# Attention steps, output blocks and the sums of h in the first channel product of batches 3 to 7, written in another order

## The chip, the core and the metric

The kernel runs on one core of one Trainium2 chip. The metric is the device time in microseconds (us) of one execution. The core has a matrix engine (PE), a vector engine (DVE), an activation engine (ACT), a general engine (POOL) and the engine whose queue issues the DMAs (SP). The engines run their own instruction lists in order and wait for each other with semaphores.

## What is computed

A block-diagonal attention, then a token and channel mixer, then a gated spatial mixer, on 8 batches of 576 tokens and 512 channels, in float32:

```python
scores = scale * np.matmul(q_c, k_c.transpose(0, 1, 2, 4, 3))     # chunks of 64 tokens, 8 heads
attn = softmax(scores); x = np.matmul(attn, v_c)
h = np.maximum(xt @ w_tok1, 0.0) @ w_tok2                         # over tokens, 576 -> 256 -> 576
u = x + h.transpose(0, 2, 1)
u + np.maximum(u @ w_ch1, 0.0) @ w_ch2                            # over channels, 512 -> 1536 -> 512
h = np.maximum(x @ w_in, 0.0); u, v = h[..., :512], h[..., 512:]
v_n = (v - mu) / np.sqrt(var + 1e-06)
v_s = np.einsum('ts,bsd->btd', w_spatial, v_n) + b_spatial[None, :, None]
(u * v_s) @ w_out
```

Every product keeps float32 accuracy: each operand is held as two float16 parts, hi and lo, and each product is three matmuls (hi·hi, hi·lo, lo·hi).

## The kernel before

The batches are worked through one after the other, and each batch has these stages on PE: the **first channel product** (`ch1`, 512 to 1536 channels), the **second** (`ch2`), the **gate stage** (five `gate_v` blocks of 128 tokens, normalised, and four `gate_u` blocks between them), the token product of the next batch (`tok1`, `tok2`), and the spatial product (`spatial`, four blocks). The **output product** of a batch (`proj`, L938, 4 or 5 blocks of 12 matmuls with 512 columns) is made in the next batch, at places where PE would else wait. The **attention** of the next batch runs beside all of it: five groups of 128 tokens (the last has 64), each of 20 small steps.

In batches 3 to 7 (`FIRST_FULL`) both channel products use Strassen's form as Winograd has it, with 7 products in place of 8. `ch1_fast(full, between)` goes through six pairs `p` of channel blocks; iteration `p` holds, in this order on PE, the products A11 and S2 of pair p, S4 and A22 of the pair before, then S1, S3 and A12 of pair p, then, if `between` names p, one output block. A product is 6 matmuls of 288 columns. A bank `a` holds A11 + A12 and, beside it, S2; a bank `d` holds S1 and S3, into which S4 and A22 are added later. So S4 of a pair may start only when DVE has read S1 and S3 out of `d`: at L732 (`vb`) and L733 (`c22`).

After A22, DVE adds the last term for two of the four blocks of h (L713, `c`). ACT applies the relu (L716; L735 and L743 for the other two blocks). `ch2_fast` needs h in seven forms: the four blocks h11, h12, h22, h21 and sums of them. DVE makes these sums at L719 (`t13`, two of them in one instruction) and L720, L721 (`t24`), and `split` makes hi (ACT, L509) and lo (POOL, L510; DVE for the first block) of each. The working tiles share three buffers. PSUM has four double banks, which the products, the output blocks and the attention share; a product waits until somebody has read its bank out.

`ch2_fast` begins with A11 of its two halves q (into banks `ab[q]`); ACT copies the result (`s1b`, L778), and only then may A12 be added into the same bank. It ends with `p34(1)`: DVE (L813) makes the residual sum, ACT (L768) its hi, DVE (L769) its lo, into `xb`, which `gate_v` reads next.

What sets the order: PE's order is written out by hand. The attention steps are issued by a pump: each matmul adds its duration times a factor, `PACE` of the stage, to a clock `slow`, and a step is issued each time the clock has gone 112 us over the number of steps. A step puts its PE part there at once (the scores, L241; the weighted sum of v, L287), and gives its DVE, ACT, POOL and DMA parts to a scheduler, which orders those engines' lists when the kernel is built, with `high_priority` blocks first. Of the attention, DVE has per group the reduce and subtract of the scores (L248, L249), the sums and the norm (L258 to L261), lo of q and k (L232) and of v (L276); ACT has hi of q and k (L229), exp (L253), hi of the probabilities (L266), of v (L273), and the two reads of the bank (L302, L303); POOL has two lo's (L269, L306).

In a gate block ACT applies the relu (L871), DVE makes the statistics (L877, L879, L884), POOL a power (L885), DVE the rest (L886, L887, L890), ACT hi (L893). A `gate_u` block's bank is read by ACT (L920).

Of the kernel before, what the change touches and what calls it, by code (L numbers as in the profile page):

```python
# [10 lines left out]
AF = mybir.ActivationFunctionType  # L11
ALU = mybir.AluOpType
# [14 lines left out]
def mixer_kernel(ctx: ExitStack, tc, qk0, qk, v, wt1, wt2, wc1, wc2, win, wsp, bsp, wout, out):  # L27
# [474 lines left out]
            stack.enter_context(tc.issue_after(ins))  # L502
        return stack

    PACE = {"first": 0.2, "pair": 0.8, "ch1": 1.0, "ch2": 1.3, "gate": 1.0, "tok1": 1.0, "last": 0.3}
    sums = {}

    def split(t, hi, lo, eng=DVE):
# [169 lines left out]
    def new_work(name):  # L678
        return wrk.tile([128, 2, 288], F32, tag="t", name=name)
# [3 lines left out]
    def ch1_fast(full, between):  # L683
        high = tc.high_priority
        ab, cd = {}, {}

        def product(o, p, n, b, start):
            w = weights_of(1, p, n, 0)
            fast_product(o, w, lambda e, k: b[:, e, k], start, True, start)

        def block(p, j):
            return hb[:, p, 0, j], hb[:, p, 1, j]

        def store(c, hi, lo, eng=POOL):
            ACT.activation(out=c, in_=c, func=AF.Relu)
            split(c, hi, lo, eng)

        for p in range(7):
            pace[0] = PACE["first" if p < 1 else "pair"]
            if p < 6:  # L700
                ab[p] = a = new_bank()
                product(a[:, 0], p, A11, xb[:, :, 0:2, T1], True)
                product(a[:, 1], p, S2, tq[1], True)
                with high():
                    ACT.activation(out=s1b[0], in_=a[:, 0, 0:288], func=AF.Copy)
                    DVE.tensor_tensor(out=u2b[p % 2], in0=a[:, 1, 0:288], in1=s1b[0], op=ALU.add)
            if p:
                d, u, xp = cd[p - 1], u2b[(p - 1) % 2], xs[(p - 1) % 2]
                product(d[:, 0], p - 1, S4, xb[:, :, 2:4, T2], False)
                product(d[:, 1], p - 1, A22, tq[3], False)  # L710
                with high():
                    c = xp[:, 1:4:2] if full else new_work("c")
                    DVE.tensor_tensor(out=c, in0=d[:, :, 0:288], in1=spread(u), op=ALU.add)  # L713
                    if full:
                        f = hF[p - 1]
                        ACT.activation(out=c, in_=c, func=AF.Relu)  # L716
                        split(xp[:, 2:4], f[:, 1:3, 0], f[:, 1:3, 1], POOL)
                        t13, t24 = new_work("t13"), new_work("t24")
                        DVE.tensor_tensor(out=t13, in0=xp[:, 1:3], in1=xp[:, 0:2], op=ALU.subtract)  # L719
                        DVE.tensor_tensor(out=t24[:, 0], in0=xp[:, 2], in1=t13[:, 0], op=ALU.subtract)  # L720
                        DVE.tensor_tensor(out=t24[:, 1], in0=xp[:, 3], in1=t24[:, 0], op=ALU.subtract)  # L721
                        split(t13, f[:, 3:5, 0], f[:, 3:5, 1], POOL)
                        split(t24, f[:, 5:7, 0], f[:, 5:7, 1], POOL)
                    else:
                        store(c, hb[:, p - 1, 0, 1:3], hb[:, p - 1, 1, 1:3])
            if p < 6:
                cd[p] = d = new_bank()
                c22 = xs[p % 2][:, 2] if full else c22b[p % 2]
                product(d[:, 0], p, S1, tq[0], True)
                product(d[:, 1], p, S3, tq[2], True)  # L730
                with high():
                    DVE.tensor_tensor(out=vb, in0=d[:, 0, 0:288], in1=u2b[p % 2], op=ALU.add)  # L732
                    DVE.tensor_tensor(out=c22, in0=d[:, 1, 0:288], in1=vb, op=ALU.add)  # L733
                    if full:
                        ACT.activation(out=c22, in_=c22, func=AF.Relu)  # L735
                    else:
                        store(c22, *block(p, 3))
                product(a[:, 0], p, A12, xb[:, :, 2:4, T1], False)
                with high():
                    x1 = a[:, 0, 0:288]  # L740
                    if full:
                        xp = xs[p % 2][:, 0]
                        ACT.activation(out=xp, in_=x1, func=AF.Relu)  # L743
                        split(xp, hF[p][:, 0, 0], hF[p][:, 0, 1], DVE)
                    else:
                        hi, lo = block(p, 0)
                        ACT.activation(out=hi, in_=x1, func=AF.Relu)
                        DVE.scalar_tensor_tensor(out=lo, in0=x1, scalar=0.0, in1=hi, op0=ALU.max, op1=ALU.subtract)
            if p in between:
                between[p]()  # L750

# [240 lines left out]
    with tc.manual_schedule(engines={mybir.EngineType.PE}):  # L992
# [12 lines left out]
        for b in range(B):  # L1005
            x = xTs[b % 2]
            if b == 0:
                pumps[0][1] = 1700.0
            def sum_next():
                with behind():  # L1010
                    todo_sums.pop(0)()

            if b == FIRST_FAST - 1:
                sum_pump([(1, p, vall) for p in range(6)], 2200.0)
            pace[0] = PACE["ch1"]
            for m in range(12 if b < FIRST_FAST else 0):
                if b == 0:
                    w_until(4 + m // 2)
                ch1(m)
            if b >= FIRST_FAST:  # L1020
                early = pend[:2]
                pend = pend[2:]
                ch1_fast(b >= FIRST_FULL, {5 - 3 * k: (lambda i=i: proj(b - 1, i)) for k, i in enumerate(early)})
            pace[0] = PACE["ch2"]
            if b == 0:
                SP.dma_start(out=bB, in_=bsp)
                ACT.activation(out=bB, in_=bB, func=AF.Copy, scale=2.0 ** -5)
            if b == FIRST_FULL - 1:
                sum_pump([(2, p, vall) for p in range(4)], 2000.0)
            if b >= FIRST_FULL:  # L1030
                ch2_fast(x)
            else:
                for ms in ((0, 1), (2,), (3,)) if b == 0 else ((0,), (1,), (2,), (3,)):
                    if b == 0:
                        w_until(10)
                    last = ch2(ms, x)
            if b == FIRST_FAST - 1:
                sum_end()
                stream(SLOTS)
            if b == 0:  # L1040
                w_until(21)
                pumps.pop(0)
                mark = last
                pumps.append([clock[0], 4000.0, held_tick, lambda: wdone[0] < len(W), clock])
            for i in pend[:2]:
                proj(b - 1, i)
            if b == FIRST_FULL - 1:
                sum_end()
                sum_pump([(2, p, hall) for p in range(4, 6)], 4500.0)
            fin = None  # L1050
            pair = [psum1(), psum1()] if b == 0 else []
            for ks in ((0, 1, 2), (3,)):
                for j, ps in enumerate(pair):
                    gate_v_part(ps, j, ks)
            pace[0] = PACE["gate"]
            middle = 0 < b < B - 1
            for n, j in enumerate((0, 4, 1, 2, 3) if middle else range(5)):
                f = gate_v(j, pair[j] if j < len(pair) else None)
                if fin:
                    fin()  # L1060
                fin = f
                if middle and n:
                    gate(n - 1)
            if middle:
                fin()
            if b == B - 1:
                fin()
            if not middle:
                for m in range(4):
                    gate(m)  # L1070
            if b < B - 1:
                a_until(b + 1)
                pumps[:] = pumps[1:]
                pace[0] = PACE["tok1"]
                last = tok1()
                attention_from(b + 2, 0.0, 112000.0)
                if b == 0:
                    with tc.issue_after(last):
                        fin()
                pace[0] = PACE["last"]  # L1080
                for m in range(4):
                    tok2(m, xTs[(b + 1) % 2], fast=b + 1 >= FIRST_FAST)
            for i in pend[2:]:
                proj(b - 1, i)
            for m in range(4):
                gated(m, b, DVE if m == 3 and b == B - 1 else POOL)
            if b == FIRST_FULL - 1:
                sum_end()
            if b < B - 1:
                w_until(len(W))  # L1090
                pend = list(range(5 if b % 2 else 4))
# [59 lines left out]
```

## Time and profile before

| | us |
|---|---|
| median of 3 runs | 1165.6 (1165.21 to 1168.64) |
| the profiled execution | 1165.78 |
| its span, first to last instruction | 1164.0 |
| PE busy in it | 1092.1 (94%) |
| DVE, ACT, POOL busy | 776.7, 506.0, 427.8 |

The share of the span lies at 94% on PE, and a busy PE is not yet PE at its peak, since a matmul's record lasts longer than the distance to the next one. So what is to be read is where PE sat idle and what ended the wait.

### The profile page before, as it was taken

The page shows a single profiled execution, that of the slowest core. Times are in us where ns is not written, and L with a number is a line of the kernel's source. Part 1 is how long each engine was busy: PE and PEld are TensorE (multiplying, and loading weights), DVE is VectorE, ACT ScalarE, POOL GpSimd, SP SyncE. Part 2 cuts the span into 40 slices and gives each one's busy share as a digit, 9 for nine tenths or more (in the row PEclk, how much of TensorE's full clock was granted, in tenths as well). Part 3 has the DMA queues.
Part 4 walks back from the last instruction along what each step waited for, and adds up shares of the span by engine and source line. Part 5 has one row for each costly group of instructions (what it writes and reads, how often), then busy time and mean ns, then how long its engine had stood idle before and what let it go on. Part 6 is the DMA issues. An engine that isn't in the chain of part 4 may idle for free.

```text
span 1164.0 us, 26575 instructions
## 1 busy us (share of the span) xinstructions
PE 1092.1 (94%) x10860; PEld 769.7 (66%) x10860; DVE 776.7 (67%) x1269; ACT 506.0 (43%) x884; POOL 427.8 (37%) x392
## 2 busy tenths in 40 slices
PE   5898999999999999988999799987999899999998
PEld 4576757776677755766667575665757676676765
DVE  7999886766565477786568846677556864467332
ACT  3334443534345244563445634455344643346131
POOL 0000032443253453653235533456234552256221
PEclk9899999999999999999999999999999999999999
DMA  9488720564046442456514674246732565124301
GB/s 318 141 250 259 231 73 19 142 160 123 19 115 176 97 114 59 115 143 199 145 39 122 168 200 110 56 132 168 196 101 48 153 153 142 19 84 140 104 19 46
DMA packets 191818, 148.36 MB, mean 127 GB/s; under 512 B 107344, under 2 KB 175696, under 8 KB 189392
## 3 DMA queue, kind: packets, MB, share of 16 engines
q1 hardware_dynamic: 191696, 146.66, 45.4%
q8 instruction: 85, 1.39, 0.5%
q14 instruction: 37, 0.30, 0.1%
HBM read 112.00 MB, written 20.45 MB: 114 GB/s over the span
## 4 chain that ended last, share of the span: by engine, by line
PE 60%; DVE 23%; ACT 5%; issue 5%; DMA 4%; POOL 2%; SPq 1%; DVEq 0%; ACTq 0%; POOLq 0%
PE mp L457 23%; PE mp L667 17%; PE mp L861 7%; PE mp L938 5%; PE mp L835 3%; PE mp L480 3%; DVE t L720 3%; DVE t L721 2%; DVE gb L154 2%; DVE gb L150 1%; DVE qk L232 1%; PE mp L241 1%; PE mp L287 1%; DMA c2s<-vn 1%; DVE gb L148 1%
## 5 line engine op out<-in xcount | busy, mean ns | idle before, releaser
L667 PEld LDWEIGHTS <-c1w 128*128 128x128 f16 x2772 | 269.8, 98 | 110.8 <-issue 40.4
L667 PE MATMUL mp<-xb,c1w 128*128 128x288 f16 x864 | 125.9, 286 | 24.6 <-DVE vn L733 10.7
L835 PE MATMUL mp<-hb,c2w 128*128 128x288 f16 x864 | 110.3, 286 | 4.2 <-DVE c2w L163 2.7
L457 PE MATMUL mp<-spw,vn 128*128 128x288 f16 x896 | 112.8, 286 | 0.0
L457 PEld LDWEIGHTS <-vn 128*128 128x128 f16 x896 | 86.9, 98 | 22.8
L835 PEld LDWEIGHTS <-c2w 128*128 128x128 f16 x864 | 82.8, 98 | 26.7 <-DVE c2w L163 4.0
L667 PE MATMUL mp<-hb,c1w 128*128 128x288 f16 x630 | 90.5, 287 | 9.3 <-ACT vn L778 8.9
L457 PE MATMUL mp<-xb,inw 128*128 128x288 f16 x768 | 98.9, 286 | 0.0
L938 PE MATMUL mp<-otw,gb 128*128 128x512 f16 x432 | 97.3, 379 | 0.0
L861 PE MATMUL mp<-inw,xb 128*128 128x512 f16 x384 | 91.0, 385 | 4.9 <-ACT xb L542 3.5
L457 PEld LDWEIGHTS <-inw 128*128 128x128 f16 x768 | 75.0, 98 | 23.6 <-issue 0.4
L667 PE MATMUL mp<-c2w,c1w 128*128 128x288 f16 x630 | 90.4, 288 | 0.0
L457 PE MATMUL mp<-xb,c1w 128*128 128x288 f16 x576 | 74.8, 290 | 4.4 <-DVE xb L536 2.5
L938 PEld LDWEIGHTS <-gb 128*128 128x128 f16 x432 | 42.2, 98 | 46.4
L457 PEld LDWEIGHTS <-c1w 128*128 128x128 f16 x576 | 56.3, 99 | 20.4 <-issue 2.9
L861 PEld LDWEIGHTS <-xb 128*128 128x128 f16 x384 | 37.3, 99 | 48.1 <-ACT xb L542 4.5
L667 PE MATMUL mp<-c1w 128*128 128x288 f16 x432 | 65.2, 286 | 0.0
L269 POOL TENSOR_TENSOR p<-sd,p 128x512 f16<-128x512 f32 (+1 forms) x30 | 38.9, 1298 | 66.4 <-ACT p L266 55.6
L928 POOL TENSOR_TENSOR gb<-gt,gb 128x576 f16<-128x576 f32 x31 | 41.1, 1327 | 60.2 <-ACT gb L927 60.2
L543 POOL TENSOR_TENSOR xb<-rt,xb 128x576 f16<-128x576 f32 x7 | 10.7, 1533 | 140.1 <-ACT xb L542 140.1
L877 DVE BATCH_NORM_STATS2 st<-vt 128x6 f32<-128x512 f32 (+1 forms) x40 | 27.5, 690 | 45.8 <-ACT vt L871 41.0
L885 POOL TENSOR_TENSOR y<-z,mhalf 128x1 f32<-128x1 f32 (+1 forms) x40 | 24.1, 602 | 92.0 <-DVE z L884 70.0
(236 smaller groups left out, 2018.6 us busy)
## 6 DMA issues: line engine op xcount, KB each, us to landing
c1w<-c1s SPq DMA_DIRECT2D x252, 128.0 KB, 2.4
c1w<-c2s SPq DMA_DIRECT2D x210, 128.0 KB, 2.4
qk<-in_qk SPq DMA_DIRECT2D x96, 128.0 KB, 2.8
out<-o SPq DMA_DIRECT2D x31, 256.0 KB, 2.0
v<-in_v SPq DMA_DIRECT2D x56, 128.0 KB, 2.9
vn<-in_wc SPq DMA_DIRECT2D x4, 1024.0 KB, 4.9
otw<-in_wc SPq DMA_DIRECT2D x3, 1024.0 KB, 4.9
spw<-in_wc SPq DMA_DIRECT2D x3, 1024.0 KB, 5.2
```

Source lines behind the costliest of these rows:

```text
L154: DVE.scalar_tensor_tensor(out=t, in0=w[:, :, 0], scalar=29, in1=t, op0=ALU.logical_shift_right, op1=ALU.bitwise_or)
L269: POOL.tensor_tensor(out=p_hl[rows, 1], in0=m["sd"][rows], in1=p_hl[rows, 0], op=ALU.subtract)
L457: PE.matmul(out=o, lhsT=l, rhs=r, start=(i == 0), stop=(i == len(seq) - 1))
L480: PE.matmul(out=pss[m], lhsT=l, rhs=r, start=(i + j == 0), stop=False)
L667: PE.matmul(out=o[:, 0:288], lhsT=w[:, a, k], rhs=b(e, k), start=(start and k + i == 0), stop=(stop and k == 1 and i == 2), skip_group_che ...
L720: DVE.tensor_tensor(out=t24[:, 0], in0=xp[:, 2], in1=t13[:, 0], op=ALU.subtract)
L835: PE.matmul(out=o, lhsT=c2w[:, a, k, mc], rhs=hb[:, k // 2, r, k % 2 * 2 + t], start=(k + e == 0), stop=(k == 11 and e == 2))
L861: PE.matmul(out=ps, lhsT=l, rhs=r, start=(k + e == 0), stop=(k == 3 and e == len(seq) - 1))
L877: keep("d", DVE.bn_stats(out=st[0:n], in_=t[0:n]))
L885: POOL.tensor_tensor(out=y[0:n], in0=z[0:n], in1=mhalf[0:n], op=ALU.pow)
L928: eng.tensor_tensor(out=gl, in0=t, in1=gh, op=ALU.subtract)
L938: PE.matmul(out=ps, lhsT=gb[:, l, k, tk], rhs=otw[:, r, k], start=(k == 0 and e == 0), stop=(k == 3 and e == 2))
```

## The change

```diff
-    PACE = {"first": 0.2, "pair": 0.8, "ch1": 1.0, "ch2": 1.3, "gate": 1.0, "tok1": 1.0, "last": 0.3}
+    PACES = ({"first": 0.2, "pair": 0.8, "ch1": 1.0, "ch2": 1.3, "gate": 1.0, "tok1": 1.0, "last": 0.3},
+             {"first": 0.0, "pair": 0.2, "ch1": 1.0, "ch2": 1.95, "gate": 1.85, "tok1": 1.5, "last": 0.0})
+    PACE = dict(PACES[0])
...
-                    c = xp[:, 1:4:2] if full else new_work("c")
+                    c = new_work("c")
                     DVE.tensor_tensor(out=c, in0=d[:, :, 0:288], in1=spread(u), op=ALU.add)
                     if full:
                         f = hF[p - 1]
-                        ACT.activation(out=c, in_=c, func=AF.Relu)
+                        ACT.activation(out=xp[:, 1:4:2], in_=c, func=AF.Relu)
+                        t13, t24 = new_work("t13"), new_work("t24")
+                        relu_less = dict(scalar=0.0, op0=ALU.max, op1=ALU.subtract)
+                        DVE.scalar_tensor_tensor(out=t13[:, 0], in0=c[:, 0], in1=xp[:, 0], **relu_less)
+                        DVE.tensor_tensor(out=t24[:, 0], in0=xp[:, 2], in1=t13[:, 0], op=ALU.subtract)
+                        DVE.scalar_tensor_tensor(out=t24[:, 1], in0=c[:, 1], in1=t24[:, 0], **relu_less)
+                        DVE.tensor_tensor(out=t13[:, 1], in0=xp[:, 2], in1=xp[:, 1], op=ALU.subtract)
                         split(xp[:, 2:4], f[:, 1:3, 0], f[:, 1:3, 1], POOL)
-                        t13, t24 = new_work("t13"), new_work("t24")
-                        DVE.tensor_tensor(out=t13, in0=xp[:, 1:3], in1=xp[:, 0:2], op=ALU.subtract)
-                        DVE.tensor_tensor(out=t24[:, 0], in0=xp[:, 2], in1=t13[:, 0], op=ALU.subtract)
-                        DVE.tensor_tensor(out=t24[:, 1], in0=xp[:, 3], in1=t24[:, 0], op=ALU.subtract)
...
+                    hi, lo = (hF[p][:, 0, 0], hF[p][:, 0, 1]) if full else block(p, 0)
+                    ACT.activation(out=hi, in_=x1, func=AF.Relu)
                     if full:
-                        xp = xs[p % 2][:, 0]
-                        ACT.activation(out=xp, in_=x1, func=AF.Relu)
-                        split(xp, hF[p][:, 0, 0], hF[p][:, 0, 1], DVE)
...
+                        ACT.activation(out=xs[p % 2][:, 0], in_=x1, func=AF.Relu)
+                    DVE.scalar_tensor_tensor(out=lo, in0=x1, scalar=0.0, in1=hi, op0=ALU.max, op1=ALU.subtract)
...
+            PACE.update(PACES[b >= FIRST_FULL])
...
-                early = pend[:2]
-                pend = pend[2:]
-                ch1_fast(b >= FIRST_FULL, {5 - 3 * k: (lambda i=i: proj(b - 1, i)) for k, i in enumerate(early)})
+                full = b >= FIRST_FULL
+                places = (1, 3, 5, 6) if full else (2, 5)
+                early, pend = pend[:len(places)], pend[len(places):]
+                ch1_fast(full, {k: (lambda i=i: proj(b - 1, i)) for k, i in zip(places, early)})
...
-            for i in pend[:2]:
+            for i in pend[:0 if b >= FIRST_FULL else 2]:
                 proj(b - 1, i)
...
-                pace[0] = PACE["last"]
+                pace[0] = PACES[b + 1 >= FIRST_FULL]["last"]
...
-            for i in pend[2:]:
+            for i in pend[0 if b >= FIRST_FULL else 2:]:
                 proj(b - 1, i)
```

The change has three parts. **The paces**: in batches 3 to 7 the attention's clock stands still in `tok2`, `spatial` and the first pair, goes at 0.2 in the other pairs, and faster in `ch2` (1.95) and the gate stage (1.85). **The output blocks**: four of them stand behind iterations 1, 3, 5 and 6 of `ch1_fast`; before, two stood behind iterations 2 and 5, and two between `ch2` and the gate stage. **The sums of h**: `c` stays as it is before the relu, two of the sums take the maximum with zero themselves, the sums are four instructions of 288 columns in place of three, and of the first block hi is made straight from the bank and lo from bank and hi. Line numbers of the changed kernel are 1 to 4 higher (L706 is L708, L713 is L715, L719 to L721 became L721 to L724, L732 and L733 are L736 and L737, L778 is L779, L813 is L814).

On DVE, the second pair of batch 3, from the sum of `a` (L706) on. The kernel before (`vn` and `xs` hold c22 and the blocks, `t13` and `t24` the sums, `mp` is a bank):

```order
L706 TENSOR_TENSOR vn_97<-mp_6361,vn_97 128x288
L713 TENSOR_TENSOR vn_97<-mp_6331,vn_97 128x2x288
L719 TENSOR_TENSOR t13_6398<-vn_97 128x576
L732 TENSOR_TENSOR vn_97<-mp_6407,vn_97 128x288
L720 TENSOR_TENSOR t24_6399<-vn_97,t13_6398 128x288
L733 TENSOR_TENSOR xs_100<-mp_6407,vn_97 128x288
L721 TENSOR_TENSOR t24_6399<-vn_97,t24_6399 128x288
L510 TENSOR_TENSOR hb_95<-xs_100,hb_95 128x288
```

The same place in the changed kernel:

```order
L708 TENSOR_TENSOR vn_97<-mp_6264,vn_97 128x288
L715 TENSOR_TENSOR c_6295<-mp_6219,vn_97 128x576
L721 SCALAR_TENSOR_TENSOR t13_6298<-c_6295,vn_97 128x288
L722 TENSOR_TENSOR t24_6299<-vn_97,t13_6298 128x288
L736 TENSOR_TENSOR vn_97<-mp_6310,vn_97 128x288
L723 SCALAR_TENSOR_TENSOR t24_6299<-c_6295,t24_6299 128x288
L737 TENSOR_TENSOR xs_100<-mp_6310,vn_97 128x288
L724 TENSOR_TENSOR t13_6298<-vn_97 128x288
L749 SCALAR_TENSOR_TENSOR hb_95<-mp_6264,hb_95 128x288
```

Ahead of the read of S3 (L733, now L737) there stood two sums that need ACT's relu; now three stand there, none of which needs it, and the one that does (L724) stands behind.

On PE, the end of `ch2` in batch 3 (its last matmul has L667, then L669; `gb` and `otw` are the output product's operands, `xb` the gate's). Before:

```order
L667 LDWEIGHTS c1w_78
L667 MATMUL mp_7126<-c2w_79,c1w_78 128x288
L938 LDWEIGHTS gb_98
L938 MATMUL mp_7387<-otw_82,gb_98 128x512
L938 LDWEIGHTS gb_98
```

and in the changed kernel:

```order
L669 LDWEIGHTS c1w_78
L669 MATMUL mp_7077<-c2w_79,c1w_78 128x288
L862 LDWEIGHTS xb_94
L862 MATMUL mp_7326<-inw_80,xb_94 128x512
L862 LDWEIGHTS xb_94
```

The two output blocks (24 matmuls) that stood between `ch2` and the first gate block are gone from there.

On DVE, the first gate block of batch 3 (`st`, `mv`, `z`, `e`, `y` are its statistics). Before:

```order
L877 BN_STATS st_7451<-vt_7449 128x6
L879 BN_AGGR mv_7453<-st_7451 128x2
L884 TENSOR_SCALAR z_7455<-mv_7453 128x1
L886 SCALAR_TENSOR_TENSOR e_7457<-y_7456,z_7455 128x1
L887 SCALAR_TENSOR_TENSOR y_7456<-e_7457,y_7456 128x1
L890 TENSOR_SCALAR vt_7449<-vt_7449,mv_7453,y_7456 128x512
L874 TENSOR_TENSOR vt_7474<-mp_7462,vt_7474 64x512
L877 BN_STATS st_7478<-vt_7474 64x6
```

and in the changed kernel:

```order
L878 BN_STATS st_7397<-vt_7395 128x6
L880 BN_AGGR mv_7399<-st_7397 128x2
L885 TENSOR_SCALAR z_7401<-mv_7399 128x1
L248 TENSOR_REDUCE mx_7526<-mp_7410 128x8
L887 SCALAR_TENSOR_TENSOR e_7403<-y_7402,z_7401 128x1
L249 TENSOR_TENSOR sd_7527<-mp_7410,mx_7526 128x2x4x64
L888 SCALAR_TENSOR_TENSOR y_7402<-e_7403,y_7402 128x1
L232 TENSOR_TENSOR qk16_86<-qk32_85,qk16_86 128x1024
L891 TENSOR_SCALAR vt_7395<-vt_7395,mv_7399,y_7402 128x512
L875 TENSOR_TENSOR vt_7473<-mp_7408,vt_7473 64x512
L258 TENSOR_REDUCE mx_7620<-sd_7527 128x8
L259 TENSOR_SCALAR mx_7620<-mx_7620 128x8
```

The steps of an attention group (L248, L249, L232, L258 and on) now stand among the statistics of the first two gate blocks.

## Rows read from the trace of the kernel before

**Rows 1.** The page: the chain that ended last, by engine and by line.

```profile
PE 60%; DVE 23%; ACT 5%; issue 5%; DMA 4%; POOL 2%; SPq 1%; DVEq 0%; ACTq 0%; POOLq 0%
PE mp L457 23%; PE mp L667 17%; PE mp L861 7%; PE mp L938 5%; PE mp L835 3%; PE mp L480 3%; DVE t L720 3%; DVE t L721 2%; DVE gb L154 2%; DVE gb L150 1%; DVE qk L232 1%; PE mp L241 1%; PE mp L287 1%; DMA c2s<-vn 1%; DVE gb L148 1%
```

**Rows 2.** Line 667 on PE: who ended its idle time, us in all, times.

```profile
  DVE vn L733: 10.7, 13
  ACT vn L778: 8.9, 5
  DVE xs L733: 5.4, 6
  DVE vn L706: 5.2, 5
  ACT xh L303: 3.4, 2
  DVE t L784: 0.3, 1
```

**Rows 3.** Waits: waiting line, releaser, us in all, times, longest.

```profile
PE mp L241 <- ACT xh L303: 1.2, 1, 1.2
```

**Rows 4.** Timeline, batch 3, first pair's end: start, us, engine, line, [idle before].

```profile
487.91 0.76 DVE L713 TENSOR_TENSOR xs<-mp,vn 128x576 f32<-128x576 f32 x1 [0.57 <-PE mp L667]
488.70 0.68 ACT L716 ACTIVATE xs<-xs 128x576 f32<-128x576 f32 x1 [1.85 <-DVE xs L713]
...
490.18 1.28 POOL L510 TENSOR_TENSOR hb<-xs,hb 128x576 f16<-128x576 f32 x1 [4.01 <-ACT hb L509]
...
490.53 1.25 DVE L720 TENSOR_TENSOR t<-xs,t 128x288 f32<-128x288 f32 x1
...
491.70 0.44 DVE L733 TENSOR_TENSOR vn<-mp,vn 128x288 f32<-128x288 f32 x1
...
492.20 0.90 PE L667 MATMUL mp<-xb,c1w 128*128 128x288 f16 x6 [0.65 <-DVE vn L733]
```

**Rows 5.** Timeline of DVE, batch 3: two operations, the second needing the first.

```profile
484.09 0.46 DVE L732 TENSOR_TENSOR vn<-mp,vn 128x288 f32<-128x288 f32 x1
484.58 0.46 DVE L733 TENSOR_TENSOR xs<-mp,vn 128x288 f32<-128x288 f32 x1
```

**Rows 6.** Timeline of PE, batch 3: a wait for attention's bank, one behind A11.

```profile
516.79 0.90 PE L667 MATMUL mp<-xb,c1w 128*128 128x288 f16 x6 [1.68 <-ACT xh L303]
...
530.57 1.26 PE L667 MATMUL mp<-hb,c1w 128*128 128x288 f16 x9 [2.95 <-ACT vn L778]
```

**Rows 7.** Line 667 on PE in 1032 to 1073 us, batch 7: who ended idle time.

```profile
  DVE vn L733: 1.8, 3
  DVE xs L733: 1.4, 1
```

**Rows 8.** Timeline of PE, batch 2: the first gate block.

```profile
421.23 0.61 PE L861 MATMUL mp<-inw,xb 128*128 128x512 f16 x2 [0.90 <-ACT xb L542]
423.27 0.54 PE L861 MATMUL mp<-inw,xb 128*128 128x512 f16 x1 [1.44 <-DVE xb L543]
```

**Rows 9.** Timelines of PE and ACT, batch 3: gate stage, its start, a relu, a later block.

```profile
565.35 2.75 PE L861 MATMUL mp<-inw,xb 128*128 128x512 f16 x12
...
581.75 3.10 PE L457 MATMUL mp<-xb,inw 128*128 128x288 f16 x24
...
580.31 0.63 ACT L920 ACTIVATE hb<-mp 128x576 f32<-128x576 f32 x1
```

**Rows 10.** Groups by line: busy us and mean ns of one, then idle time before.

```profile
L232 DVE TENSOR_TENSOR qk<-qk,qk 128x1024 f16<-128x1024 f32 (+1 forms) x30 | 39.2, 1305 | 0.4 <-ACT qk L229 0.4
L261 DVE TENSOR_TENSOR sd<-sd,mx 128x512 f32<-128x512 f32 (+1 forms) x30 | 25.0, 834 | 0.9
L248 DVE TENSOR_REDUCE mx<-mp 128x8 f32<-128x512 f32 (+1 forms) x30 | 20.5, 682 | 8.8 <-PE mp L241 8.7
L229 ACT ACTIVATE qk<-qk 128x1024 f16<-128x1024 f32 (+1 forms) x30 | 29.1, 969 | 10.1 <-PE mp L241 10.1
```

More of the change, by code (lines that the diff above doesn't have):

```diff
@@ L740, in ch1_fast @@
                     x1 = a[:, 0, 0:288]
+                    hi, lo = (hF[p][:, 0, 0], hF[p][:, 0, 1]) if full else block(p, 0)
+                    ACT.activation(out=hi, in_=x1, func=AF.Relu)
                     if full:
-                        xp = xs[p % 2][:, 0]
-                        ACT.activation(out=xp, in_=x1, func=AF.Relu)
-                        split(xp, hF[p][:, 0, 0], hF[p][:, 0, 1], DVE)
[L745 to L748, printed above, removed]
+                        ACT.activation(out=xs[p % 2][:, 0], in_=x1, func=AF.Relu)
+                    DVE.scalar_tensor_tensor(out=lo, in0=x1, scalar=0.0, in1=hi, op0=ALU.max, op1=ALU.subtract)
             if p in between:
```

## The prediction

> **What bounds the kernel now.** I read first the page's chain of work that ended last, then who ended the idle time of the line that makes both fast channel products, then one pair in the timeline. The chain is 60% PE and 23% DVE, and two of DVE's lines on it, L720 and L721, are sums of h [rows 1]; so PE is the bound, and the first channel product (`ch1`) is where something else runs ahead of it. Line 667 waited 32 times, for 33.9 us together [rows 2]. The idle times are a little short: a product of 6 matmuls is recorded with 0.90 us, of which the last lasts about 0.286, so the distance is (0.90 - 0.286)/5 = 0.123 us, and each wait costs 0.286 - 0.123 = 0.16 us more than is written. So 33.9 + 32 x 0.16 = 39.1 us, and with the score matmul that waited for attention's bank [rows 3] 1.2 + 0.16 more: **40.5 us** in which PE waits in `ch1` and at the head of `ch2`. This is all that the change can win there; the rest of PE's work keeps its count of matmuls.
>
> How a pair waits is seen in [rows 4]. c is added (L713, 487.91), ACT's relu follows at 488.70, and POOL begins a lo at 490.18 for 1.28 us, until 491.46. DVE's L720 starts at 490.53, has 288 columns, for which L733 takes 0.44 us, but lasts 1.25 and ends at 491.78, 0.32 us after POOL's. It reads and writes SBUF alone; L733, which reads a bank, runs in full beside the next lo. So a DVE sum out of SBUF stands still as long as POOL makes a lo, and L733 is queued behind it: it ends at 492.14, and PE's S4, which adds into the bank that L733 reads, starts at 492.20 in place of 492.20 - 0.65 - 0.16 = 491.39. That is 3.48 us behind L713: the time that DVE has.
>
> **The sums of h.** Removed is the wait for ACT's relu ahead of the sums; added is one DVE instruction per pair (30 in all, some 0.45 us each), on a DVE that has 5.1 us per pair (7 products of 6 x 0.123). The new order from the start of c's add, by [rows 5] (0.49 us to an operation that needs the one before, 0.36 to 0.46 to one that doesn't) and 0.78 behind the add, which lasts 0.76: L721 at 0.78, L722 at 1.27, L736 at 1.63 to 1.73, L723 at 2.0 to 2.2, L737 at 2.4 to 2.6, done by 2.8 to 3.1. That is ahead of 3.48, so S4 doesn't wait. POOL's lo still comes 490.18 - 487.91 = 2.27 us behind the add, since relu and hi on ACT ahead of it are as before, and L723 begins just ahead of it. If L723 comes too late, it is held until 2.27 + 1.28 = 3.55, ends at 3.9, L737 ends at about 4.3, and the wait is 0.8 us as it was.
>
> The rows show that DVE stands still beside POOL's lo, whichever of the pair's sums it is. The Trainium skill (SBUF — State Buffer, "SBUF: two separate sides") has it as an exclusive lock on a port pair that the two share, for a DVE operation with two SBUF inputs too: whichever starts first keeps it for the whole instruction. By that rule four locked sums per pair in place of three speak against the change, and a lead of 0.1 to 0.3 us decides; it is the rival "lost race" below.
>
> **The output blocks.** A block is 12 matmuls of 512 columns; twelve of that size are recorded with 2.75 us [rows 9], 2.6 from start to start, 0.216 each. Behind iterations 1, 3 and 5 it gives L737 3.48 + 2.6 us, so even a lost race costs nothing there; iterations 2 and 4 have none, which leaves 2 pairs in each of 5 batches open. The block behind iteration 6 stands between the last A22 and `ch2`: the wait behind A11 there, 2.95 + 0.16 us [rows 6], is for L778, queued on ACT behind hi of the last sums; 2.6 us of block and 0.8 us that the sums start earlier (no relu ahead) cover it, also the other four of its kind, which are shorter. What the two blocks left bare is the way from `ch2` to the gate: DVE's sum, ACT's hi, DVE's lo, about 0.2 + 0.76 + 0.7 + 0.76 = 2.4 us and some gaps, against 9 matmuls of 0.216 (1.9 us) that need none of it, and two more ahead of the one that needs lo (2.4). So I take 0.1 us for each of five batches, 0.5 in all. The bound from the other side is batch 2, where the first gate block waited 0.90 and 1.44 us [rows 8] though two blocks stood ahead: 2.7 us with the correction, in five batches 13.
>
> **The attention.** The order keeps one score and one weighted sum in `ch1` (iterations 3 and 5); the ones from `spatial` went to `ch2` and the gate. So of the waits, those for L303 (3.4 + 1.2, and 0.16 each) and for L706, L733 behind attention's DVE steps go if the rest of the steps are out of the way. The measure is batch 7, which has no attention: four waits, 3.2 us [rows 7], all for L733, which the sums and blocks remove. I leave 0.3 us per batch for what stays, 1.5 in all; at most two waits like the 1.68 [rows 6] in each of four batches would be 15.
>
> Paid is this in the gate stage. There a block waits for the bank that ACT's relu L920 of an earlier one reads: L920 ended at 580.94, PE needed it at 581.75 [rows 9], 0.8 us to spare. Ahead of that relu the order now has one group's L248, L249 (as long), L232, L258 (as long) and L261 among the statistics: 0.68 + 0.68 + 1.3 + 0.68 + 0.83 = 4.2 us [rows 10], some of it where DVE waited for POOL's power anyway, so 2.5 to 4.2. PE comes there about 0.8 us later itself, with a score and a sum more ahead. 2.5 to 4.2, less 1.6, is 0.9 to 2.6; I take 1.6, in batches 3, 4 and 5 (batch 6 has fewer groups left, and none ahead of that relu): **5 us**, from 0 to 8.
>
> **Sum.** 40.5 - 1.5 - 0.5 - 5 = 33.5 us. The profiled execution took 1165.78, 0.2 above the median: 1165.78 - 33.5 = 1132.
>
> **The rivals.**
> - *Lost race*: POOL's lo begins ahead of L723. 10 pairs x 0.8 to 0.9 us, 9 us back: 1141. For it: the lead is 0.1 to 0.3 us; against it: every step ahead of POOL's is unchanged.
> - *Bare gate*: the first gate block waits as in batch 2 [rows 8]: 13 us back, 1145. Against it: batch 2's residual is one piece of 576 columns behind other work on DVE, and the new order has sum, lo and copy on DVE in a row.
> - *It doesn't do what it says*: the group that is left in `ch1` keeps making the waits for L706, L778 and L303: 5.2 + 8.9 + 3.4 + 1.2 + 13 x 0.16 = 20.8 us stay, 1153.
> - *The gate becomes the bound, slower than before*: two groups' DVE work per batch (twice some 5 us, from 4.2 and lo of v) and ACT's beside it (L229 alone 0.97) come whole into the line from relu to statistics to relu of the five gate blocks, and PE waits for their banks. It is slower than before from 10 us per batch in four batches on, which eats the 40; with 13 it is 1165.8 - 40.5 + 52 = 1177. Against it: DVE is busy for 776.7 of 1164 us, and the gate had 0.8 us to spare at its tightest.
>
> **How the numbers follow.** The forecast (1124 to 1138, by the gate's 0 to 8 us and nothing left or 3 us left in `ch1`) 0.58; lost race 0.20; bare gate 0.09; not what it says 0.08; slower 0.05. The predicted time is 1132. The range reaches to the lost race and the bare gate: 1123 to 1147, which leaves out about 0.17. A measurement can tell some 0.3% (3.5 us) from no change: faster by more than that 0.94 (the first four cases but 0.01), within it 0.02 (that 0.01, and as much of the last case, just at its point), slower 0.04.
>
> **What would show it.** Right: in the changed trace the waits of the fast product's line for L737 are few, those for L779 and L303 gone, and a gate_u block in batches 3 to 5 waits for its relu L921 by one to two us. L722 and L723 last about 0.45 us, not 1.2. Wrong: waits for L737 of 0.8 us in iterations 3 and 5 (lost race), waits of the gate's first block for L769 or L770 (bare gate), waits for L303 inside `ch1`.

## The result

The changed kernel takes 1176.3 us (median of 4 runs, 1175.31 to 1177.38), the kernel before 1165.6: ratio 1.0086, 95% interval 1.0067 to 1.0106. It is **0.9% slower**; the forecast was 1132, range 1123 to 1147. The profiled execution took 1176.0 us, its span is 1174.0. Lines of the changed kernel are 1 to 4 higher than in the kernel before; L732/L733 are now L736/L737, L778 is L779, L920 is L921.

The waits of PE, then the one of ACT that matters (waiting line, releaser, us in all, times, longest), answer [rows 2, 3]:

```profile
PE mp L241 <- ACT vt L872: 9.1, 3, 3.6
PE mp L457 <- ACT hb L921: 8.9, 3, 3.1
...
PE mp L669 <- ACT vn L779: 7.3, 4, 2.3
PE mp L669 <- DVE c2w L749: 6.7, 3, 2.2
...
PE mp L669 <- DVE vn L737: 1.4, 2, 1.0
...
PE mp L862 <- DVE xb L770: 1.3, 3, 0.6
...
ACT qk L229 <- DMA qk<-in_qk: 26.4, 6, 6.5
```

Most of what the change was to remove is gone: L733's waits, 16.1 us in [rows 2], are 1.4 as L737's, and L303 and L706 are no longer in the list. The wait at the head of the second product stays: L779 has 7.3 us in 4, where [rows 2] have 8.9 in 5 for L778. New are one wait in the first product (L749) and two in the gate stage (L872, L921), each once in batches 3, 4 and 5. Of L229's six waits for its load, three stand in the gate stages of these batches (5.85, 6.51 and 5.21 us), the other three in `ch2`. Batch 3 by stages; columns are the stretch, its length, the busy time of PE, PEld, DVE, ACT, POOL, the granted clock of PE (1.00 is 2.4 GHz, a half is 1.2), the share of DMA and GB/s. First the gate stage before, then `ch1`, `ch2` and the gate stage after:

```profile
565.30:590.20 24.90, 24.90 (x225) 15.45 (x224) 14.16 (x37) 11.95 (x21) 8.09 (x10) 1.00 0.36 104
```

```profile
477.90:524.40 46.50, 44.29 (x398) 30.87 (x396) 33.49 (x59) 27.18 (x54) 23.96 (x20) 0.96 0.54 144
524.40:561.80 37.40, 35.11 (x421) 26.92 (x420) 21.52 (x37) 13.46 (x24) 13.85 (x13) 0.95 0.72 190
561.80:596.80 35.00, 28.60 (x322) 17.10 (x321) 22.63 (x51) 15.68 (x27) 11.55 (x14) 0.90 0.47 125
```

The gate stage is 10.1 us longer. Its matmuls are the same but for 96 small ones of the attention, a score and a weighted sum that moved in from the stages behind it; 48 of them take 0.50 us, so about 1 us is this work. This table adds up such stretches for batches 3 to 7 (`ch1` and `ch2` are taken together, since the blocks move from one to the other):

| batches 3 to 7, us | `ch1`+`ch2` | gate | the rest | sum |
|---|---|---|---|---|
| before | 416.3 | 123.3 | 140.1 | 679.7 |
| after | 399.1 | 155.2 | 136.9 | 691.2 |
| forecast's change | -39.0 | +5.5 | 0 | -33.5 |
| measured change | -17.2 | +31.9 | -3.2 | +11.5 |

(The forecast's columns are 40.5 - 1.5 and 0.5 + 5. Ahead of batch 3 the changed kernel was 1.5 us earlier, so the span grew by 10.0.)

**The gate.** ACT's timeline there, in batch 3 (start, us, line, [idle before]), and PE's:

```profile
565.66 0.60 ACT L872 ACTIVATE vt<-mp 128x512 f32<-128x512 f32 x1
572.12 1.06 ACT L229 ACTIVATE qk<-qk 128x1024 f16<-128x1024 f32 x1 [5.85 <-DMA qk<-in_qk]
573.08 0.61 ACT L253 ACTIVATE sd<-sd 128x512 f32<-128x512 f32 x1
573.72 0.59 ACT L874 ACTIVATE vt<-mp 64x512 f32<-64x512 f32 x1
```

```profile
582.04 0.57 PE L241 MATMUL mp<-qk 64*64 64x64 f16 x48 [3.09 <-ACT vt L872]
582.54 0.60 PE L862 MATMUL mp<-inw,xb 128*128 128x512 f16 x2
586.27 5.20 PE L457 MATMUL mp<-xb,inw 128*128 128x288 f16 x24 [3.12 <-ACT hb L921]
```

ACT stands for 5.85 us at L229, the hi of the next group's q and k, because their load has not landed. L874, the read of a gate block, was ready and queued behind it; in the kernel before it began at 569.92 in a gate stage that started 3.5 us later. The Trainium skill (Perfetto Trace Analysis, "Tensor Engine Instruction (MATMUL, LD_WEIGHTS)") says that ACT, DVE and GpSimd take their queues strictly in order; the trace agrees, 5.85 us long. DVE stands too: lo of the same q and k (L232) waits for it, and the first gate block's L891 is queued behind L232:

```profile
573.21 1.23 DVE L232 TENSOR_TENSOR qk<-qk,qk 128x1024 f16<-128x1024 f32 x1 [4.26 <-ACT qk L229]
574.35 0.54 DVE L891 TENSOR_SCALAR vt<-vt,mv,y 128x512 f32<-128x512 f32 x1
```

All that follows on ACT and DVE is late, and PE waits twice for a bank; the 24 matmuls behind the second wait took 5.20 us where [rows 9] have 3.10.

Why the load was late is on the SP queue:

```profile
562.58 0.49 SPq L218 DMA_DIRECT2D qk<-in_qk  x1
563.16 2.02 SPq L594 DMA_DIRECT2D c1w<-c1s  x3
565.23 0.49 SPq L218 DMA_DIRECT2D qk<-in_qk  x1
...
569.23 0.47 SPq L218 DMA_DIRECT2D qk<-in_qk  x1
```

The buffer was free from 557.8 on (L232 had read it), but the load's four parts were issued from 562.58 to 569.23, between loads of weights. A part lands 2.8 to 3.5 us after its issue; L229 starts at 572.12, 2.9 us behind the issue of the last.

**The first product.** One wait each of batches 3 to 5 is for the bank of x1, which the new sums let DVE read last (L749):

```profile
503.11 1.65 DVE L276 SCALAR_TENSOR_TENSOR v<-v,v 128x512 f16<-128x512 f32 x1 [0.41 <-ACT v L273]
...
504.68 0.45 DVE L749 SCALAR_TENSOR_TENSOR c2w<-mp,c2w 128x288 f16<-128x288 f32 x1
...
505.18 1.09 PE L669 MATMUL mp<-xb,c1w 128*128 128x288 f16 x4 [2.21 <-DVE c2w L749]
```

L749 stands behind attention's lo of v. The wait that stayed is at the head of `ch2`:

```profile
523.64 1.48 DVE L261 TENSOR_TENSOR sd<-sd,mx 128x512 f32<-128x512 f32 x1
...
525.05 0.75 DVE L715 TENSOR_TENSOR c<-mp,vn 128x576 f32<-128x576 f32 x1
...
526.46 1.23 DVE L722 TENSOR_TENSOR t<-vn,t 128x288 f32<-128x288 f32 x1
...
531.26 1.02 PE L669 MATMUL mp<-hb,c1w 128*128 128x288 f16 x7 [2.29 <-ACT vn L779]
```

The last c (L715) came behind five DVE steps (L232, L258 to L261) of the one group left in `ch1`, and the sums behind it met POOL again (L722: 1.23 us, not 0.45).

In the pairs themselves POOL's lo often began ahead of L723: in 10 of its 30 runs L723 took 1.16 to 1.53 us, not 0.45. In six of them L737 was queued behind it, each time while PE made an output block; in batch 7, with PE's block from 1068.18 to 1070.93:

```profile
1068.79 1.28 POOL L512 TENSOR_TENSOR hb<-xs,hb 128x576 f16<-128x576 f32 x1 [1.06 <-ACT hb L511]
1068.88 1.50 DVE L723 SCALAR_TENSOR_TENSOR t<-c,t 128x288 f32<-128x288 f32 x1
```

### The profile page after: what moved, and what is told of

Read it like the earlier page. It is cut to its first block, busy times and chain, and to the rows that moved or that the text cites. A ratio compares the mean times of both kernels' runs of the same rounds, so it can differ in the third digit from the quotient of the medians.

```text
span 1174.0 us, 26626 instructions
## 1 busy us (share of the span) xinstructions
PE 1100.7 (94%) x10860; PEld 774.0 (66%) x10860; DVE 771.0 (66%) x1299; ACT 501.8 (43%) x884; POOL 424.5 (36%) x392
## 4 chain that ended last, share of the span: by engine, by line
PE 62%; DVE 20%; DMA 5%; ACT 5%; issue 3%; POOL 3%; SPq 1%; ACTq 0%; DVEq 0%; POOLq 0%
PE mp L669 23%; PE mp L457 22%; PE mp L939 5%; PE mp L862 4%; PE mp L836 3%; PE mp L480 3%; DVE gb L154 2%; DVE gb L150 1%; DMA qk<-in_qk 1%; DVE qk L232 1%; DVE gb L148 1%; DVE c L715 1%; PE mp L241 1%; DMA c2s<-vn 1%; DVE sd L261 1%
## 5 line engine op out<-in xcount | busy, mean ns | idle before, releaser
L669 PEld LDWEIGHTS <-c1w 128*128 128x128 f16 x2772 | 272.1, 99 | 94.3 <-issue 19.1
L669 PE MATMUL mp<-xb,c1w 128*128 128x288 f16 x864 | 127.4, 287 | 8.1 <-DVE c2w L749 6.7
L457 PE MATMUL mp<-xb,inw 128*128 128x288 f16 x768 | 104.9, 296 | 9.5 <-ACT hb L921 8.9
L457 PEld LDWEIGHTS <-inw 128*128 128x128 f16 x768 | 77.4, 101 | 38.0 <-issue 11.8
L669 PE MATMUL mp<-hb,c1w 128*128 128x288 f16 x630 | 91.8, 291 | 8.5 <-ACT vn L779 7.3
L669 PE MATMUL mp<-c2w,c1w 128*128 128x288 f16 x630 | 92.3, 292 | 0.0
L669 PE MATMUL mp<-c1w 128*128 128x288 f16 x432 | 66.1, 288 | 0.0
L895 POOL TENSOR_TENSOR vn<-vt,vn 128x512 f16<-128x512 f32 x32 | 37.8, 1183 | 61.9 <-ACT vn L894 61.9
```

The source lines that it names most:

```text
L457: PE.matmul(out=o, lhsT=l, rhs=r, start=(i == 0), stop=(i == len(seq) - 1))
L669: PE.matmul(out=o[:, 0:288], lhsT=w[:, a, k], rhs=b(e, k), start=(start and k + i == 0), stop=(stop and k == 1 and i == 2), skip_group_che ...
L895: POOL.tensor_tensor(out=vn[:, 2 * j + 1], in0=t, in1=vn[:, 2 * j], op=ALU.subtract)
```

## The experiments

Theory A: the loss in the gate is the load of q and k on the SP queue. Its rival, B: it is the attention's own work there. Theory C: the first product's new wait is DVE's late read of x1's bank. First the three parts of the change, each alone, and two together. The kernel before, measured again beside each experiment, took 1167.8 to 1168.2 (1165.6 beside the changed kernel), so a difference of 2 or 3 us between rows is better read from the ratios.

| kernel | us | ratio to before, 95% interval | `ch1`+`ch2` | gate |
|---|---|---|---|---|
| after | 1176.3 | 1.0086 [1.0067, 1.0106] | 399.1 | 155.2 |
| sums alone | 1156.5 | 0.9917 [0.9896, 0.9938] | 408.6 | 123.3 |
| blocks alone | 1165.0 | 0.9975 [0.9958, 0.9992] | 403.1 | 134.3 |
| paces alone | 1179.5 | 1.0112 [1.0089, 1.0135] | 414.5 | 141.2 |
| sums and blocks | 1150.9 | 0.9857 [0.9833, 0.9881] | 391.6 | 132.7 |
| after, second buffer | 1154.7 | 0.9893 [0.9869, 0.9917] | 398.9 | 134.6 |
| after, loads first | 1157.6 | 0.9909 [0.9881, 0.9938] | 395.6 | 140.7 |
| after, old gate density | 1161.4 | 0.9946 [0.9930, 0.9963] | 382.8 | 150.7 |
| after, x1 from `xs` | 1170.5 | 1.0028 [1.0006, 1.0050] | 389.8 | 156.3 |
| second buffer and old gate density | 1138.1 | 0.9736 [0.9714, 0.9758] | 380.5 | 129.7 |
| the same, x1 from `xs` | 1136.3 | 0.9722 [0.9704, 0.9741] | 380.4 | 128.4 |
| sums and blocks, second buffer | 1149.5 | 0.9842 [0.9819, 0.9866] | 390.8 | 132.6 |
| sums, three blocks moved | 1157.9 | 0.9921 [0.9896, 0.9946] | 406.3 | 123.4 |

**Sums alone** (the two hunks of the diff in `ch1_fast`). 

> The kernel before with the new sums of h alone; output blocks and the placing of the attention as before. Theory A (the sums do what the forecast said, the loss is all in where the attention went): the waits that L733 ended (13 and 3 + 1 in batch 7, 0.65 us each) go, 10 to 14 us faster, 1152 to 1156. Theory B (the sums themselves cost the new waits of the first product, because DVE's L749 now reads the bank of x1 that ACT alone read before): waits of about 2 us for L749 come in each of the batches 3 to 6, with a stretch of half clock behind each, and the time is 1160 to 1168.

1156.5, about 10 us faster: theory A's gain, at its small end, and its mechanism in part. The waits for the read of S3 (L735 here) fall from 16.1 us to 6.4, in 10 waits, and do not go. One that stays, in batch 7, which has no attention, is the lost race: POOL's lo begins 0.10 us ahead of the shared sum (L721 here), and no output block covers it:

```profile
1052.69 1.28 POOL L510 TENSOR_TENSOR c2w<-vn,c2w 128x576 f16<-128x576 f32 x1 [1.06 <-ACT c2w L509]
1052.79 1.49 DVE L721 SCALAR_TENSOR_TENSOR t<-c,t 128x288 f32<-128x288 f32 x1
...
1054.70 0.90 PE L667 MATMUL mp<-xb,c1w 128*128 128x288 f16 x6 [0.98 <-DVE xs L735]
```

The fast products wait nowhere for L747 (L749 in the changed kernel), only two score matmuls do, 1.9 us together; so the bank read alone doesn't make the wait. What stays is the head of `ch2`: 10.3 us in 4 waits for ACT's copy, where [rows 2] have 8.9 in 5.

**Blocks alone** (`places = (1, 3, 5, 6)`, none behind `ch2`). 

> The kernel before with four output blocks in the first channel product (behind iterations 1, 3, 5 and 6) and none behind the second, and nothing else. Theory A: the waits for L778 at the head of the second product (8.9 us, 5) go under the block behind iteration 6, and the gate's first block waits under 1 us per batch: 4 to 8 us faster, 1158 to 1162. Theory B (the blocks leave the gate bare): the first gate block of batches 3 to 7 waits 1 to 2.5 us for the residual and the half clock follows, within 2 us of the time before or slower.

1165.0, 0.25% faster than before, a time between the two theories'; the gate is as B has it, since its first block waits 4.9 us in 3 for the residual's hi and 1.5 in 3 for its lo. `ch1` and `ch2` are 13.2 us shorter and the gate 11.0 longer, in batches 3 to 5 by 4.3, 1.8 and 4.5.

**Paces alone** (the `PACES` hunk and its two uses). 

> The kernel before with the new places of the attention steps alone. Theory A (the loss is made in the gate stage, by steps that follow each other too closely there: the copy of q and k, L229, is reached before their load has landed): L229 waits for its DMA some 5 us once per batch in batches 3, 4 and 5, the gate stage of these is 8 to 10 us longer as in the changed kernel, and the waits for L303, L706 and part of those for L733 in the first product go (some 15 us): 1172 to 1185. Theory B (the loss comes from all three parts meeting): the gate stage is no more than 3 us longer per batch and the time is 1145 to 1160.

1179.5, and A's mechanism: L229 waits for its load in the three batches.

```profile
ACT qk L229 <- DMA qk<-in_qk: 17.4, 3, 6.7
ACT qk L229 <- DMA c1w<-c1s: 5.7, 2, 4.0
```

The gate stage is 6 us longer, less than A said (8 to 10); the gain expected in `ch1` hardly came (1.8 us with `ch2`), since the old sums still waited there, and PE had new waits for its weights' load (c1w<-c2s: 6.3 us, 3 times).

**Sums and blocks**, the attention where it was. 

> The changed kernel with the places of the attention steps as before: new sums and new output blocks alone. Theory A: the gate stage of batches 3 to 5 is 25 us long as before, L229 waits for no load, the waits that L733 and L778 ended go by two thirds: 1142 to 1152. Theory B (the sums and blocks make the loss in the first product whatever the attention's place): the waits for L749 and for ACT's copy at the head of the second product are as in the changed kernel or longer, 1158 to 1168.

1150.9, theory A. So the whole loss came with the attention's move: 25 us lie between this kernel and the changed one. Its gate stage is still 1.8 to 4.3 us longer than before, and its traces of ACT and PE tell why:

```profile
563.78 0.63 ACT L266 ACTIVATE p<-sd 128x512 f16<-128x512 f32 x1 [2.40 <-DVE sd L261]
564.32 0.68 ACT L767 ACTIVATE xb<-w 128x576 f16<-128x576 f32 x1
```

```profile
565.05 0.60 PE L860 MATMUL mp<-inw,xb 128*128 128x512 f16 x2 [1.80 <-ACT xb L767]
```

The residual's hi, L767, is queued behind an attention step that waits for DVE. This was read, not tried.

**A second buffer** for q and k, their load one group (five steps) earlier; to make room, half of `tq4` went to a free piece of the weights' tile. Nothing else moves.

```diff
-    qk32 = new("qk32", [128, 2, 4, 128], F32)
+    qk32s = new("qk32", [128, 2, 2, 4, 128], F32)
...
-            [lambda: at_load_qk(g)], [], [qk_hi], [qk_lo], [], [score],
+            [load], [], [qk_hi], [qk_lo], [], [score],     # load: at_load_qk(g + 1); the first group also its own
```

> The changed kernel with a second buffer for q and k in float32 and their load issued five attention steps earlier; all work and all other places as in the changed kernel. Theory A (the gate's loss is L229 on ACT, held by the load of q and k, with everything of the gate queued behind it on ACT): L229's waits for the load in batches 3 to 5 (26.4 us, 6) go, PE's waits for ACT's L872 and L921 (9.1 and 8.9 us, 3 each) and the half clock behind them go, the gate stage falls from 35 to 25 to 27 us: 1148 to 1156. Theory B (the loss is the attention's own work in the gate, whatever is loaded when): the gate stage stays over 31 us, 1164 to 1176.

1154.7, 21.6 us less than the changed kernel; the gate stage gives 20.6. The only waits of ACT's L229 (here L235) are for PE, and one wait of PE in batch 3's gate is left:

```profile
ACT qk L235 <- PE mp L247: 4.2, 6, 1.5
```

```profile
580.46 3.10 PE L467 MATMUL mp<-xb,inw 128*128 128x288 f16 x24 [1.81 <-ACT hb L931]
```

The gate stage is 28.3 to 28.4 us in batches 3 to 5, a little over A's 27. Theory A is shown, B falls: all the attention's work is still there. Of the 3.4 us per batch that remain, about 1 is the attention's own matmuls on PE and 1.8 to 2.0 is this wait (5.7 us in 3).

**The loads first**: one buffer, the four parts of the load in a `high_priority` block, which sets them together on the SP queue. 

> The changed kernel with the four loads of q and k set ahead of what else is ready on the SP queue; one buffer, all other places the same. Theory A1 (the load is late because its four pieces stand between weight loads and transposes, 562.6 to 569.2, though the buffer is free from 557.8): issued in one go they land some 3 us behind the last, L229 waits under 2 us per batch, the gate stage is 26 to 30 us, 1152 to 1162. Theory A2 (two steps at 1.85 are too short for a load of 3.1 us wherever it stands in the queue): L229 waits 4 us or more per batch, the gate stage is over 31 us, 1165 to 1178.

```profile
561.44 3.19 SPq L218 DMA_DIRECT2D qk<-in_qk  x4
564.73 5.28 SPq L598 DMA_DIRECT2D c1w<-c1s  x9
```

1157.6, A1: L229's waits for the load fall from 26.4 us to 4.1 (2 times), the gate stage to 30.1 to 30.6, a little over A1's 30. It was the place in the queue that made the load late, more than the distance between the steps.

**The old gate density** (`"gate": 1.0, "tok1": 1.0, "last": 0.3` in the second row of `PACES`), old buffer. 

> The changed kernel with the gate, tok1 and tok2 as dense in attention steps as before (1.0, 1.0, 0.3 in place of 1.85, 1.5, 0.0); first product and second product as in the changed kernel. Theory A (two steps lie between the load and L229, and at 1.85 they follow each other too fast in the gate for the load to land): L229 waits under 2 us there, the gate stage is 25 to 28 us, what stays are the first product's waits for L749 and L779: 1148 to 1158. Theory B (the load is late because the SP queue has it among the weight loads, whatever the distance): L229 waits 4 us or more per batch and the gate stage stays over 31 us: 1164 to 1176.

1161.4, between the two, and A's reason was wrong. The wait for the load didn't go, it moved to the end of `ch2`, where the residual's hi (L769) is queued behind it:

```profile
562.73 1.06 ACT L229 ACTIVATE qk<-qk 128x1024 f16<-128x1024 f32 x1 [4.58 <-DMA qk<-in_qk]
563.69 0.61 ACT L253 ACTIVATE sd<-sd 128x512 f32<-128x512 f32 x1
564.21 0.67 ACT L769 ACTIVATE xb<-w 128x576 f16<-128x576 f32 x1
```

```profile
564.93 1.46 PE L862 MATMUL mp<-inw,xb 128*128 128x512 f16 x3 [5.61 <-ACT xb L769]
```

The gate stage stays 32 to 35 us long. What it won is in `ch1` and `ch2`, 16.3 us, where the steps now stand at places without the waits for L749 and L779.

**x1 from `xs`**: lo of h's first block as before. 

> The changed kernel with lo of h's first block made as before from xs in SBUF, so that the bank of x1 is free when ACT has read it and not when DVE has (L749). Theory C (the first product's new wait, 2.2 us in batches 3 to 5, is the bank's last reader standing on DVE behind attention's L276): the wait falls to 1 us or less, the half clock behind it (3.4 us) goes in these three batches: 4 to 9 us faster than the changed kernel, 1167 to 1172. Rival (ACT's read of the same bank stands as late behind the attention's L273 and L302): the wait stays 1.5 us or more, 1174 to 1178.

1170.5, about 6 us less than the changed kernel: theory C. The wait of 2.21 us is now this, without the lower clock behind it:

```profile
504.30 0.90 PE L669 MATMUL mp<-xb,c1w 128*128 128x288 f16 x6 [0.18 <-ACT vn L747]
```

**Both, second buffer and old gate density.** 

> The changed kernel with both: the second buffer for q and k with the earlier load, and the gate as dense in attention steps as before (1.0, 1.0, 0.3). Theory A (with the old buffer and this density the wait for the load only went from the gate to the end of the second product, where it holds the residual's hi, L769, 4.6 to 7.5 us; with the second buffer nothing is held): PE's wait for L769 falls from 7.0 to under 1.5 us, the gate stage from 33 to 25 to 27 us, the first product stays at 42 to 43 us: 1135 to 1143. Rival (the first gate block is bare whatever the load does, and ACT's other steps stand there): 2 to 3 us of wait and the half clock stay in each gate: 1144 to 1151, no better than sums and blocks alone.

1138.1, 2.6% faster than before; theory A. Batch 3's gate stage again:

```profile
558.40:585.00 26.60, 25.27 (x226) 15.34 (x225) 15.75 (x40) 11.77 (x21) 7.65 (x10) 1.00 0.53 125
```

Over five batches `ch1` and `ch2` are 35.8 us shorter than before (forecast: 39.0) and the gate 6.4 longer (forecast: 5.5).

**The same with x1 from `xs`.** 

> The kernel with the second buffer and the old gate density, and lo of h's first block made from xs in SBUF as before. Theory C (DVE's late read of the bank of x1 costs only where an attention group's DVE steps stand ahead of it in iteration 3; with the old gate density none does): within 2 us of the kernel with the bank read. Rival (the read out of the bank costs in every batch): 4 to 9 us faster than that kernel.

1136.3; the two intervals overlap, so no difference is shown: where no attention step stands ahead of it, the bank read costs less than these runs resolve. It is theory C's second half.

**Sums and blocks with the second buffer.** 

> New sums and new output blocks with the attention's places as before, and the second buffer with the earlier load. Theory A (the buffer is worth something only where the moved attention reaches L229 before its load; moving the attention out of the first product is itself a gain of some 12 us once the load is covered): L229 waited for no load in this order with one buffer, so the time stays within 3 us of that kernel, 1148 to 1154. Rival (the earlier load helps by itself, and the moved attention brings nothing): 1136 to 1145, as with the attention moved.

1149.5 against 1150.9: theory A. The buffer is worth nothing by itself; with it, moving the attention is worth 11.4 us at the old gate density (1149.5 to 1138.1), and at the changed kernel's it costs 5.2 (1149.5 to 1154.7).

**Sums, and three of four blocks moved** (`places = (1, 3, 6)`, one stays behind `ch2`). 

> The new sums, and of the new output blocks those behind iterations 1, 3 and 6; the fourth stays behind the second product as before; attention as before. Theory A (in the kernel with sums and blocks alone, 1150.9, the first gate block's waits of 2.0 + 0.8 us in batches 3 and 5 and 1.4 + 0.35 in batch 4 are for a residual that one block of 2.6 us would cover): the gate stage falls from 27 to 29 us to about 25, the first product loses at most 1 us per batch: 1142 to 1149. Theory B (the block behind iteration 5 is worth as much there, by the waits for L706 and L735): 1149 to 1154.

A miss: 1157.9, 7 us slower than with all four. The gate stage is 24.9 us as expected, but the first product lost more than B allowed for. DVE and PE at the end of iteration 5 of batch 3:

```profile
518.48 0.68 DVE L249 TENSOR_TENSOR sd<-mp,mx 128x512 f32<-128x512 f32 x1
519.08 0.44 DVE L706 TENSOR_TENSOR vn<-mp,vn 128x288 f32<-128x288 f32 x1
```

```profile
519.58 0.90 PE L667 MATMUL mp<-xb,c1w 128*128 128x288 f16 x6 [1.19 <-DVE vn L706]
523.34 1.60 PE L667 MATMUL mp<-xb,c1w 128*128 128x288 f16 x6 [2.87 <-DVE vn L735]
```

Attention's L232, L248 and L249 of the group scored in this iteration stand on DVE ahead of the pair's sums. With no block behind iteration 5, S4 of iteration 6 (523.34) comes next and waits 2.87 us, and its six matmuls take 1.60 us, not 0.90. Attention is only part of it: batch 7, which has none, waits 2.45 us at the same place, with the shared sum held beside POOL ahead of the read of S3:

```profile
1061.48 1.48 DVE L721 SCALAR_TENSOR_TENSOR t<-c,t 128x288 f32<-128x288 f32 x1
...
1063.38 0.90 PE L667 MATMUL mp<-xb,c1w 128*128 128x288 f16 x6 [2.45 <-DVE vn L735]
```

Common to both is that no block covers DVE's way to that read: with one there (sums and blocks) the waits for L735 are 1.1 us in all, here 13.0.

## Why the prediction was wrong

Between forecast and measurement lie 43.5 us of the span: 26.4 in the gate and 21.8 in `ch1` and `ch2`, less 3.2 in the later stages and 1.5 ahead of batch 3.

- **The sums: right in what PE pays, wrong on the race.** The waits for L737 are 1.4 us in all. But the lost race, which had 0.20, came in a third of the pairs: L723 was to take some 0.45 us and took 1.16 to 1.53 in 10 of 30. It cost PE nothing where an output block stood, as the prediction says of these places; with the sums alone it cost 0.98 us in batch 7. At the head of `ch2` L722 was held too (1.23 us), behind a late c.
- **The blocks: nearly right here, but not for the reason given.** The first gate block waited 0.2, 0.6 and 0.9 us in batches 3, 4 and 5. I counted only the residual's own steps, and took 0.1. Sums and blocks with the attention's old places lengthen the gate by 1.8 to 4.3 us: as read there, what decides is which attention step ACT has ahead of the residual's hi.
- **What stays in `ch1`: mis-sized.** I left 1.5 us by the measure of batch 7, which has no group at all. The one group left cost 6.7 us (L749) and 7.3 (L779), and a lower clock behind them: 17.2 us were won where 39.0 were forecast. I had not followed that the new lo reads x1's bank on DVE, so that whatever stands on DVE ahead of L749 holds PE. With better places for that group and the second buffer 35.8 were won: the total to be had was nearly right, not the leftover.
- **The gate: the step that failed.** Its term was 5 us, 0 to 8; it measured 31.9. I counted DVE's instructions and ACT's relu ahead of one bank, and left out what the moved steps issue elsewhere: the load on the SP queue, with weight loads between its parts, and L229 on ACT, which waits for it with the whole gate queued behind it. The second buffer takes 20.6 us of that back with all the work in place. Of the rest, about 10 us (3.4 in each of three batches), some 3 are PE's own matmuls of the moved steps, and 5.7 are the wait for the gate_u relu, which I had priced at 1.6 per batch, 5 us in all: the term was right in size, and the load was missing from it. That DVE's and ACT's attention steps make that wait was not tried. With the old density the gate is only 0.9 to 2.4 us longer.
- **The rivals.** "The gate becomes the bound, slower" had the time (1177) and the place, and 10 us per batch in three batches. The time was luck: it added 52 us in the gate to a gain of 40.5, where 31.9 and 17.2 were measured. Its mechanism was not the one: two groups' work on DVE and ACT doesn't fill that line, a load holds it up. "It doesn't do what it says" had the size in `ch1` and `ch2` (20.8 us more than the forecast stay; 39.0 - 17.2 = 21.8 did), by the group that is left there, though with L749 in place of L706 and L303, and a lower clock.
- **The clock** stood in no term. The mean granted clock of the span fell from 0.991 to 0.980: 1174.0 x 0.020 = 23.5 us short of full against 1164.0 x 0.009 = 10.5, so 13 us, part of them in idle time.

**Open:** the three parts alone multiply to 1.0003, the changed kernel is at 1.0086. Paces alone have a gate stage of 30.8 us, with blocks and sums it is 35.2. The two blocks that stood between `ch2` and the gate gave the load 5 us of PE's time; that this is the whole difference was not tried.

## To carry to other kernels

When steps are moved closer together, list for each step what it issues on every queue, loads first: where in the queue the load will stand, when its buffer comes free, and which in-order engine will stand at its first reader. A load that is late costs whatever is queued behind that reader, and slowing the steps only moves the place; a second buffer or the load's parts set together removes it. Test the parts of a change one by one: here two of three were a gain, and the third became one (1138.1) with a second buffer and the old density in the gate.

## Unexpected of the hardware

- **What a wait of 2 to 3 us costs beyond itself.** In the stretch from 579.0 to 590.5 of the changed kernel, with the two waits of 3.1 us, the granted clock was 0.71 on average (0.50, the level of 1.2 GHz, from 584 to 590), in the kernel before 1.00; 24 matmuls took 5.20 us against 3.10. Behind the wait of 2.21 us in `ch1` the stage's mean was 0.96; with the second buffer the gate's wait of 1.81 us left it at 1.00.
- **DVE beside POOL is the same outside the pairs.** L722 lasted 1.23 us while POOL made attention's lo of the probabilities. The Trainium skill (SBUF — State Buffer, "SBUF: two separate sides") has the lock for a DVE operation with two SBUF inputs against any POOL instruction that reads SBUF, and the trace agrees: 1.23 against 0.45 us.
- **A load in parts is as late as its last part.** Each part of 128 KB landed in 2.8 to 3.5 us; in the changed kernel 9.5 us passed from the first issue to the first use of all four; set in a row they are issued in 3.19 us.
